# Top-32 attention and a mixture of depths: score blocks turned and masked by half rows, and the order of a step's work on TensorE changed

## The chip, the cores and the metric

The kernel runs on one core of one Trainium2 chip. The core has five engines, each with its own queue of instructions that it works off in order: TensorE (PE in the profile; PEld is its weight loads, which overlap its products), VectorE (DVE), ScalarE (ACT), GpSimd (POOL) and SyncE (SP, which here only starts transfers). They wait for each other through semaphores. TensorE writes into PSUM, eight banks of 512 float32 values for each of 128 partitions; ScalarE and VectorE read those banks, and everything else lies in SBUF. The metric is device time in microseconds (us), as the median of several runs.

## What is computed

Two blocks, one after the other. First attention for 8 batches of 8 heads, 576 positions and 64 channels, in which each query keeps only its 32 largest scores:

```python
scores = scale * np.matmul(q, k.transpose(0, 1, 3, 2))
kth = np.partition(scores, -top_k, axis=-1)[..., -top_k:-top_k + 1]
mask = scores >= kth
scores = np.where(mask, scores, -1000000000.0)
scores = scores - np.max(scores, axis=-1, keepdims=True)
attn = np.exp(scores)
attn = attn / (np.sum(attn, axis=-1, keepdims=True) + 1e-09)
return np.matmul(attn, v).astype(np.float32)
```

The heads of a batch are laid side by side to rows of 512, and then, in each batch, 128 of the 576 rows (those with the largest product with a gate vector) go through a small two-layer network and are added to:

```python
scores = np.einsum('bsd,d->bs', x, w_gate)
out = x.copy()
for b in range(B):
    top_idx = np.argpartition(-scores[b], capacity)[:capacity]
    xe = x[b, top_idx]
    h = np.maximum(xe @ w1, 0.0)
    ye = h @ w2
    g = 1.0 / (1.0 + np.exp(-scores[b, top_idx]))
    out[b, top_idx] = x[b, top_idx] + g[:, None] * ye
```

## The kernel before, in words

The work is cut into units. A unit is one block of 128 queries for two heads (two half blocks of 64 queries for the last 64 positions, where four heads share a unit). A batch has 18 units, the whole problem 144. The scores of a unit, `sc`, are 128 partitions (queries) by 2 heads by 576 keys.

The main loop (line 1108) is a pipeline over units. In its step n five units are in work at once, each in another stage:

- unit n+1: its scores are multiplied on TensorE (`multiply`, line 486) into four PSUM banks and copied to SBUF by ScalarE (`keep`, line 506);
- unit n: VectorE finds a lower bound of the 32nd largest score (`bound_of`, line 1066);
- unit n-1: ScalarE marks what lies below the bound (`sides`, line 554) and GpSimd multiplies scores and marks into `y` (line 1080);
- unit n-2: VectorE finds the 32nd largest itself in `y` (`kth_of`, line 1084);
- unit n-3: `mask_of` (line 1102) writes `less`, bfloat16, which is positive where a score is below the 32nd largest; ScalarE does the first head, GpSimd the second;
- unit n-4: `weigh` (line 1053) turns the scores on TensorE so that keys lie on partitions, ScalarE takes the exponential (`pT`, and `last` for the last 64 keys of both heads), `values` (line 642) multiplies with v into the bank `av`, and `keep_values` (line 674) copies the result to `xs`.

Turning and masking are two products into the same place: a transpose of a 128x128 block of scores, and on top of it a product of `less` with the matrix `out_of_reach`, which has -2^90 on its diagonal, so that what is masked becomes hugely negative before the exponential (`turn_some`, line 608). A unit has eight such blocks, four for each head, in the two banks `tr`, and a ninth (`turn_last`, line 630), in the last 128 columns of the bank `av`, with the last 64 keys of both heads.

Beside this, a step on TensorE carries up to two "half loads" (blocks of the next batch's keys or queries, transposed into spare columns of the score banks, `loads`, line 1169) and, behind the values, a piece of the mixture of an earlier batch (`next(mixtures[b], None)`, line 1219): part of the first layer (`h_ps`), of the second (`y_ps`), or a transpose of the chosen rows (`xe_ps`). ScalarE's part of the mixture (`hT`, `xeT`, `gy`) is put into a list, `late`, which `flush` (line 210) empties right after the step's mask.

The order is written out by hand: each engine runs its instructions in the order of the program text (`InOrder`, line 37, which is why nearly all instructions carry line 45 in the profile). So in one step of the main loop

- TensorE does: eight blocks of turn and mask, the ninth block, the half loads' transposes, the scores of unit n+1, the values of unit n-4, a piece of the mixture;
- ScalarE does: exponential `pT`, exponential `last`, `less`, the list `late`, the copies of the half loads, the copy `sc`, the copy `xs`, `sides` twice.

The first product of the values waits for ScalarE's exponential `last`, since the block that it reads lies in the bank `av` that the values write. All eight PSUM banks are in use: two for `tr`, one for `av`, one for the mixture, four for the scores.

After the loop a hand-written ending (from line 1290) does the same for the last four units without new scores, and then the mixture of the last batch.

Of the kernel before, what the change touches and what calls it, by code (L numbers as in the profile page):

```python
# [10 lines left out]
AF = mybir.ActivationFunctionType  # L11
# [20 lines left out]
J = 4  # L32
# [16 lines left out]
def kernel(  # L49
# [16 lines left out]
    NHP = H // 2  # L66
    NT = J + 1
    JP = J * P
    R = S - JP
# [4 lines left out]
    scale = 1.0 / float(D) ** 0.5 / SMALLER  # L74
# [29 lines left out]
    ident = const.tile([P, P], FP32, name="ident")  # L104
# [132 lines left out]
    class Rows:  # L237
# [67 lines left out]
        def turn_last(self, w, tr):  # L305
            for c in range(NHP):
                pe.transpose(
                    tr[:, c // 2, c % 2 * R : (c % 2 + 1) * R],
                    self.last[w][:, 2 * c : 2 * c + 2, :].rearrange("p h d -> p (h d)"),
                    ident[0:R, 0:R],  # L310
                )
# [14 lines left out]
        def turn(self, i, tr, c0=0, c1=J):  # L326

            for c in range(c0, c1):
                pe.transpose(
                    tr[:, c - c0, :],  # L330
                    self.rows[i][:, c, :, :].rearrange("p h d -> p (h d)"),
                    ident,
                )
            if c1 == J:
                self.fetch()
# [144 lines left out]
    def room_for_scores():  # L480
        return ps_sc.tile([P, 2, 2, 512], FP32, name="ps")
# [21 lines left out]
    def by_head(ps):  # L503
        return [ps[:, i, :, :] for i in range(2)]
# [103 lines left out]
    def turn_some(tr, z, less):  # L608

        pe.transpose(tr, z, ident)  # L610
        if less is not None:
            pe.matmul(
                tr, less, out_of_reach, start=False, stop=True, skip_group_check=True
            )

    def room_to_turn():
        return ps_tr.tile([P, 2, J, P], FP32, name="ptr"), ps_av.tile(
            [P, 512], FP32, name="av"
        )

    def turn(z, tr, less=None):

        for i in range(2):
            for c in range(J):
                at = slice(c * P + i * R, (c + 1) * P + i * R)
                turn_some(
                    tr[:, i, c, :], z[:, i, at], None if less is None else less[:, i, at]
                )

    def turn_last(z, av, less=None):  # L630

# [10 lines left out]
    def values(t, g, pT, last, av, vs):  # L642

        vt, vpair = vs  # L650
        for i, heads in enumerate(heads_of(t, g)):
            for c in range(J):
                for r in (0, R):
                    h = heads[-1 if r else 0][0]
                    pe.matmul(
                        av[r : r + R, i * DE : (i + 1) * DE],
                        pT[:, i, c, r : r + R],
                        vt[:, h, c, :],
                        start=(c == 0 and i == 0),
                        stop=False,  # L660
                        skip_group_check=True,
                    )
        for r in (0, R):
            h = heads_of(t, g)[0][-1 if r else 0][0]
            pe.matmul(
                av[r : r + R, 0 : 2 * DE],
                last[:, r : r + R],
                vpair[:, h // 2, :, :].rearrange("p h e -> p (h e)"),
                start=False,
                stop=True,  # L670
                skip_group_check=True,
            )
# [377 lines left out]
    def is_unit(n):  # L1050
        return 0 <= n < N

    def weigh(sc, tr, av, less):

        turn(sc, tr, less)
        tr_last = turn_last(sc, av, less)
        pT = ptpool.tile([P, 2, J, P], FP32, name="pT")
        last = ptpool.tile([P, P], FP32, name="last")

        def exp():  # L1060
            act.activation(pT, tr, AF.Exp, scale=scale)
            act.activation(last, tr_last, AF.Exp, scale=scale)

        return pT, last, exp

    def bound_of(n):
        b, i = divmod(n, per_batch)
# [40 lines left out]
    for n in range(-1, N):  # L1108
        b, i = divmod(n, per_batch)
        if i == 0 and 0 <= b < B - 1:  # L1110
            qkv[b + 1] = room_for_qkv(b + 1)
            loading = chain(
                loading, Rows(k[b + 1], q[b + 1], *qkv[b + 1][0:2]).parts()
            )
        if 0 < n + 1 < NHP:
            first_pairs.turn(n + 1)
        if n == 0:
            for hp in range(2):
                first_pairs.turn_queries(hp)
            for hp in range(2):  # L1120
                first_pairs.keep_queries(hp)
        if n == NHP - 1:
            for hp in range(2, NHP):
                first_pairs.turn_queries(hp)
            for hp in range(2, NHP):
                first_pairs.keep_queries(hp)
            first_pairs.last_queries()
            first_steps.close()
            ps_sc = all_steps.enter_context(
                tc.tile_pool(name="ps_sc", bufs=1, space=PS)  # L1130
            )
        if n == 1:
            load_v(v[0], qkv[0][2])
        if n == NHP:
            load_weights()


        gating = normalised
        if inverting is not None:
            normalised = inverting[0:2]  # L1140
            vector_late.insert(0, lambda a=inverting: normalise(*a))
            inverting = None
        else:
            normalised = None
        if gating is not None:
            amid_late.append(lambda a=gating: gates(*a))

        if is_unit(n - 4):  # L1150
            tr, av = room_to_turn()
            pT, last, exp = weigh(scs.pop(n - 4), tr, av, masks.pop(n - 4))
            exp()
        if is_unit(n - 3):
            mask_of(n - 3, (act, None) if n in scatter_steps else None)
        flush()
        if is_unit(n + 1):
            b, t, g = units[n + 1]
            kT, qT = qkv[b][0:2]
            b, i = divmod(n, per_batch)  # L1160
            if n + 1 < NHP:
                ps = room_for_first_scores()
                multiply(t, g, kT, qT, ps)
                if is_unit(n - 1):
                    what_is_below(n - 1)
                stay_busy((10, 10, 20, 30)[n + 1])
            else:
                ps = room_for_scores()
                loads = list(islice(loading, first_loads[i] if b == 0 else loads_at[i]))
                halves = [ps[:, a, :, HALF : HALF + P] for a in range(2)]  # L1170
                for load, half in zip(loads, halves):
                    load[0](half)
                multiply(t, g, kT, qT, by_head(ps))
                for load, half in zip(loads, halves):
                    load[1](half)
                if n == NHP - 1:
                    stay_busy(20)
            scs[n + 1] = keep(ps)
        if is_unit(n - 4):
            b4, t4, g4 = units[n - 4]  # L1180
            values(t4, g4, pT, last, av, qkv[b4][2])
            if n in place_steps:
                values_bank[0] = av
                next(mixtures[place_steps[n]])
            if g4 == 0:
                xs = xpool.tile([P, H, DE], FP32, name="xs")
                if t4 == 0:
                    x = xpool.tile([P, NT, HD], FP32, name="x")
                    pg = gates_of[b4 % 2]
                    of_batch[b4] = x, pg  # L1190
            keep_values(t4, g4, av, xs)
            if g4 == groups(t4) - 1:
                inverting = b4, t4, xs
                n4 = R if t4 == J else P
                keep_sums(n4, xs, sums[0:n4, b4 * NT + t4, :])
            while kept:
                kept.pop(0)()


        if is_unit(n):  # L1200
            bound_of(n)
        flush_vector()
        flush_pool()
        if is_unit(n - 2):
            kth_of(n - 2)
        while after_kth:
            after_kth.pop(0)()


        if is_unit(n - 1) and n + 1 >= NHP:  # L1210
            what_is_below(n - 1)

        if gating is not None:
            b, t = gating
            if t == J:
                store(out[b], of_batch[b][0])
                mixtures[b] = mixture(float(b * S), of_batch[b][1], ranks[:, b, :])
        for b in mix_steps.get(n, ()):
            next(mixtures[b], None)
        b, i = divmod(n, per_batch)  # L1220
        if i == v_at and 0 <= b < B - 1:
            load_v(v[b + 1], qkv[b + 1][2])
# [14 lines left out]
    weighed = {}  # L1237
# [2 lines left out]

    def weigh_unit(m):
        tr, av = other_room(m) if (N - m) % 2 else room_to_turn()
        weighed[m] = *weigh(scs.pop(m), tr, av, masks.pop(m)), av

    def values_unit(m):
        pT, last, _, av = weighed[m]
# [371 lines left out]
```

## Time and profile before

| | |
|---|---|
| time, median of 3 runs (lowest to highest) | 814.45 us (814.24 to 816.94) |
| the profiled execution: its time, and its span | 816.28 us, 814.4 us |
| granted TensorE clock, mean | 0.998 |
| busy: PE, PEld | 777.2 us (95%), 600.3 us (74%) |
| busy: DVE, ACT, POOL | 783.5 us (96%), 729.5 us (90%), 721.6 us (89%) |
| 18 steps, from 400.00 to 495.88 us | 95.88 us; DVE busy 95.73, PE 94.83, ACT 91.08, POOL 90.47 |

The time of an execution is that of the slowest core; here there is one. The span runs from its first instruction to its last. A line of the timeline gives the start in us from the beginning of the span, the time taken, the engine, the operation, what it writes and reads, `row x column` sizes, and in brackets the idle time before it with what ended it. Products on TensorE are pipelined: each takes about 0.2 us from start to end, but the next one starts long before; their cost is read from one start to the next. A float32 product appears as two records, a float32 transpose as one. Tile names stand without their numbers: `ptr` is `tr`, `ps` the score banks, `rows` and `last` the loaded keys and queries (but `last<-av` on ScalarE is the exponential of the ninth block).

### The profile page before, as it was taken

How to read it: one execution, taken by the hardware profiler on the slowest of the kernel's cores; microseconds unless marked ns; L12 is line 12 of the kernel's file. 1: busy time of each engine (PE TensorE's matmuls, PEld its weight loads, DVE VectorE, ACT ScalarE, POOL GpSimd, SP SyncE). 2: the span in 40 equal slices, each digit the busy share in tenths (PEclk: the TensorE clock that was granted, in tenths of full speed). 3: DMA queues.
4: the chain of work that ended last, by engine and by line, in shares of the span. 5: the costliest groups of instructions: out<-in, count | busy, mean ns of one | idle time of the engine just before them, and what ended most of it. 6: DMA issues, size and time to landing. Idle time of an engine off the chain costs nothing. (4 is left out here: it accounts for less than half of the span.)

```text
span 814.4 us, 28453 instructions
## 1 busy us (share of the span) xinstructions
PE 777.2 (95%) x10231; PEld 600.3 (74%) x10231; DVE 783.5 (96%) x4655; ACT 729.5 (90%) x1577; POOL 721.6 (89%) x722
## 2 busy tenths in 40 slices
PE   8988888888999999999999999999999999999987
PEld 6766666667887778877787777877788777867756
DVE  6999999999999999999999999999999999999962
ACT  5999999999999999999999999999999999879840
POOL 3899999999999999999999999999999999998921
PEclk9999999999999999999999999999999999999999
DMA  8931214121151123221251221512224102001021
GB/s 169 287 89 28 52 58 106 29 53 28 60 114 26 43 59 90 66 54 33 74 106 29 54 41 60 100 28 54 41 80 94 28 3 79 23 5 25 2 72 30
DMA packets 121732, 50.38 MB, mean 62 GB/s; under 512 B 116016, under 2 KB 116016, under 8 KB 120560
## 3 DMA queue, kind: packets, MB, share of 16 engines
q1 hardware_dynamic: 118368, 43.94, 22.0%
q0 software_dynamic: 1744, 4.20, 2.9%
q8 instruction: 82, 1.34, 0.7%
q14 instruction: 66, 0.54, 0.2%
q10 hardware_dynamic: 1472, 0.36, 0.2%
HBM read 36.93 MB, written 11.55 MB: 60 GB/s over the span
## 5 line engine op out<-in xcount | busy, mean ns | idle before, releaser
L45 POOL TENSOR_TENSOR y<-sc,sides 128x576 f32<-128x576 f32 x288 | 365.8, 1294 | 51.0 <-ACT sides L45 49.3
L45 DVE MAX8 cand<-sc 128x8 f32<-128x82 f32 (+1 forms) x2016 | 314.0, 227 | 4.3 <-ACT sc L45 4.2
L45 POOL TENSOR_SCALAR less<-sc,next 128x576 bf16<-128x576 f32 x135 | 233.2, 1728 | 2.2 <-DVE next L45 1.2
L45 ACT ACTIVATE sides<-sc,bound 128x576 bf16<-128x576 f32 x288 | 223.5, 791 | 0.0
L45 PE MATMUL ptr<-out_of_reach,less 128*128 128x128 bf16 x1136 | 203.3, 219 | 18.0 <-POOL less L45 17.1
L45 PE MATMUL ptr<-ident,sc 128*128 128x128 f32 x1136 | 214.6, 280 | 0.0
L45 DVE MAX8 next<-y 128x8 f32<-128x584 f32 x288 | 204.4, 751 | 0.5 <-POOL y L45 0.5
L45 PEld LDWEIGHTS av<-v,pT 128*64 128x64 f32 x4608 | 146.1, 137 | 65.9 <-ACT last L45 62.6
L45 ACT ACTIVATE pT<-ptr 128x1024 f32<-128x1024 f32 x142 | 145.3, 1024 | 39.5 <-PE ptr L45 38.5
L45 PEld LDWEIGHTS ptr<-ident,sc 128*128 128x128 f32 x1136 | 159.9, 141 | 28.2 <-issue 16.7
L45 PE MATMUL ps<-kT,qT 64*128 64x288 f32 (+1 forms) x1248 | 174.0, 425 | 0.0
L45 PE MATMUL av<-v,pT 128*64 128x65 f32 x4608 | 166.0, 224 | 8.1 <-ACT last L45 7.4
L45 PEld LDWEIGHTS <-less 128*128 128x128 bf16 x1296 | 134.4, 104 | 36.7 <-POOL less L45 24.0
L45 ACT COPY sc<-ps 128x1152 f32<-128x1152 f32 x140 | 159.1, 1137 | 0.0
L45 PEld LDWEIGHTS ps<-kT,qT 64*128 64x128 f32 (+1 forms) x1248 | 95.8, 175 | 34.5 <-issue 20.9
L45 ACT ACTIVATE less<-sc,next 128x576 bf16<-128x576 f32 x141 | 109.8, 779 | 2.9 <-DVE next L45 2.8
L45 DVE MATCH_REPLACE8 cand<-best,cand 128x21 f32<-128x21 f32 (+1 forms) x576 | 98.9, 179 | 0.0
L45 DVE MAX8 best<-cand 128x8 f32<-128x21 f32 (+1 forms) x576 | 90.3, 189 | 0.0
L45 PE MATMUL h_ps<-xeT,w 128*128 128x128 f32 x464 | 65.7, 286 | 0.0
L45 PEld LDWEIGHTS h_ps<-xeT,w 128*128 128x128 f32 x464 | 55.8, 191 | 9.1 <-issue 7.0
L45 ACT ACTIVATION_READ_ACCUMULATOR sides<-sc,bound 128x1 f32 x288 | 61.0, 212 | 0.0
L45 PE MATMUL y_ps<-w,hT 128*128 128x512 f32 x112 | 60.6, 636 | 0.0
(165 smaller groups left out, 908.3 us busy)
## 6 DMA issues: line engine op xcount, KB each, us to landing
v<-in_v_dram SPq DMA_DIRECT2D x64, 128.0 KB, 4.4
out_dram<-x SPq DMA_DIRECT2D x8, 1024.0 KB, 4.0
rows<-in_k_dram SPq DMA_DIRECT2D x56, 128.0 KB, 2.9
rows<-in_q_dram SPq DMA_DIRECT2D x56, 128.0 KB, 3.0
w<-in_moe_w_dram SPq DMA_DIRECT2D x2, 2048.0 KB
gate_row<-row_dram SPq DMA_DIRECT2D x7, 288.0 KB, 4.4
last<-in_q_dram SPq DMA_DIRECT2D x8, 128.0 KB, 3.3
vpair<-in_v_dram SPq DMA_DIRECT2D x16, 64.0 KB, 3.9
```

Of the source, the lines that this page charges most:

```text
L45: return lambda *a, **kw: self._tc.keep_in_program_order(fn(*a, **kw))
```

## The change

Three things are changed, in three functions and in the main loop.

First, `turn` no longer takes a block of 128 queries whole. Each block is turned as two halves of 64 queries, partitions 0 to 63 and 64 to 127, each against its own 64x64 corner of the identity; then each half is masked with its own 64x64 corner of `out_of_reach`. A unit's eight blocks were 8 transposes and 8 masks with 128 moving columns, and are now 16 and 16 with 64 moving columns, in the order: first half turned, second half turned, first half masked, second half masked. The halves go to different PSUM banks: `by_half` reads the two banks as one for each half of the queries (before: one for each head). `values` reads the exponentials through the same view; the exponential itself is unchanged. The ninth block stays whole.

Second, the ninth block is taken out of `weigh` into a function of its own, `turn_rest`, and is turned after the scores of unit n+1. ScalarE's exponential `last` moves with it: it stood before `less` and the list `late`, and now stands behind both.

Third, the half loads' transposes, which stood before the scores of unit n+1, now follow the scores and the ninth block. So TensorE's order in a step is: eight blocks by halves, scores, ninth block, half loads, values, mixture. ScalarE's is: `pT`, `less`, `late`, `last`, half loads' copies, `sc`, `xs`, `sides`.

In the ending after the loop, blocks are turned by halves too, but the ninth block still follows at once.

```diff
+    def by_half(a):
+        return a.rearrange("p r c (b i) -> p r (c b) i", i=R)
+
     def turn(z, tr, less=None):
+        to = by_half(tr)
+        halves = [slice(r * R, (r + 1) * R) for r in range(2)]
         for i in range(2):
             for c in range(J):
                 at = slice(c * P + i * R, (c + 1) * P + i * R)
-                turn_some(
-                    tr[:, i, c, :], z[:, i, at], None if less is None else less[:, i, at]
-                )
+                for r, q in enumerate(halves):
+                    pe.transpose(to[:, r, i * J + c, :], z[q, i, at], ident[q, q])
+                for r, q in enumerate(halves):
+                    if less is not None:
+                        pe.matmul(
+                            to[:, r, i * J + c, :],
+                            less[q, i, at],
+                            out_of_reach[q, q],
+                            start=False,
+                            stop=True,
+                            skip_group_check=True,
+                        )
...
                     pe.matmul(
                         av[r : r + R, i * DE : (i + 1) * DE],
-                        pT[:, i, c, r : r + R],
+                        by_half(pT)[:, r // R, i * J + c, :],
                         vt[:, h, c, :],
...
     def weigh(sc, tr, av, less):
         turn(sc, tr, less)
-        tr_last = turn_last(sc, av, less)
         pT = ptpool.tile([P, 2, J, P], FP32, name="pT")
         last = ptpool.tile([P, P], FP32, name="last")
         def exp():
             act.activation(pT, tr, AF.Exp, scale=scale)
-            act.activation(last, tr_last, AF.Exp, scale=scale)
-        return pT, last, exp
+
+        def turn_rest():
+            tr_last = turn_last(sc, av, less)
+            return lambda: act.activation(last, tr_last, AF.Exp, scale=scale)
+
+        return pT, last, exp, turn_rest
...
                 ps = room_for_scores()
+                multiply(t, g, kT, qT, by_head(ps))
+        if is_unit(n - 4):
+            turn_rest()()
+        if is_unit(n + 1):
+            if n + 1 >= NHP:
+                b, i = divmod(n, per_batch)
                 loads = list(islice(loading, first_loads[i] if b == 0 else loads_at[i]))
                 halves = [ps[:, a, :, HALF : HALF + P] for a in range(2)]
                 for load, half in zip(loads, halves):
                     load[0](half)
-                multiply(t, g, kT, qT, by_head(ps))
                 for load, half in zip(loads, halves):
                     load[1](half)
```

More of the change, by code (lines that the diff above doesn't have):

```diff
@@ L1151 @@
             tr, av = room_to_turn()
-            pT, last, exp = weigh(scs.pop(n - 4), tr, av, masks.pop(n - 4))
+            pT, last, exp, turn_rest = weigh(scs.pop(n - 4), tr, av, masks.pop(n - 4))
             exp()
@@ L1159 @@
             kT, qT = qkv[b][0:2]
-            b, i = divmod(n, per_batch)
             if n + 1 < NHP:
@@ L1242, in weigh_unit, with both @@
         tr, av = other_room(m) if (N - m) % 2 else room_to_turn()
-        weighed[m] = *weigh(scs.pop(m), tr, av, masks.pop(m)), av
+        pT, last, exp, turn_rest = weigh(scs.pop(m), tr, av, masks.pop(m))
+        exp_rest = turn_rest()
+        def both():
+            exp()
+            exp_rest()
+        weighed[m] = pT, last, both, av
     def values_unit(m):
```

## The prediction

> **What bounds the kernel now.** I read the page's busy line first, then the windows over one batch, then the timeline of one step for TensorE and ScalarE, then the totals of the waits.
>
> ```profile
> PE 777.2 (95%) x10231; PEld 600.3 (74%) x10231; DVE 783.5 (96%) x4655; ACT 729.5 (90%) x1577; POOL 721.6 (89%) x722
> ...
> 400.00:495.88 95.88, 94.83 (x1262) 73.38 (x1263) 95.73 (x577) 91.08 (x198) 90.47 (x88) 1.00 0.27 60
> ```
>
> These are busy us of PE, PEld, DVE, ACT and POOL; the second line is one batch of 18 steps, 5.33 us a step. VectorE has 0.15 us of idle time in it, so no change elsewhere can make a batch much shorter than VectorE's own work. But VectorE isn't alone. One step on TensorE, then on ScalarE:
>
> ```profile
> 413.46 1.16 PE L45 MATMUL h_ps<-xeT,w 128*128 128x128 f32 x8
> 414.45 0.27 PE L45 MATMUL ptr<-ident,sc 128*128 128x128 f32 x1
> 414.56 0.22 PE L45 MATMUL ptr<-out_of_reach,less 128*128 128x128 bf16 x1
> 414.62 0.28 PE L45 MATMUL ptr<-ident,sc 128*128 128x128 f32 x1
> ...
> 415.76 0.22 PE L45 MATMUL ptr<-out_of_reach,less 128*128 128x128 bf16 x1
> 415.81 0.28 PE L45 MATMUL av<-ident,sc 128*128 128x128 f32 x1
> ...
> 415.99 0.39 PE L45 MATMUL ps<-ident,rows 128*128 128x128 f32 x2
> 416.30 1.24 PE L45 MATMUL ps<-kT,qT 64*128 64x288 f32 x8
> 417.47 1.15 PE L45 MATMUL av<-v,pT 128*64 128x65 f32 x32
> 418.46 0.39 PE L45 MATMUL av<-vpair,last 128*64 128x130 f32 x4
> 418.78 1.05 PE L45 MATMUL h_ps<-xeT,w 128*128 128x128 f32 x7
> ```
>
> ```profile
> 416.02 1.02 ACT L45 ACTIVATE pT<-ptr 128x1024 f32<-128x1024 f32 x1 [0.50 <-PE ptr L45]
> 416.94 0.27 ACT L45 ACTIVATE last<-av 128x128 f32<-128x128 f32 x1
> 417.09 0.78 ACT L45 ACTIVATE less<-sc,next 128x576 bf16<-128x576 f32 x1
> 417.76 0.38 ACT L45 ACTIVATE hT<-h_ps 128x256 f32<-128x256 f32 x1
> 418.02 0.39 ACT L45 ACTIVATE qT<-ps 128x256 f32<-128x256 f32 x1
> ...
> 419.28 0.31 ACT L45 COPY xs<-av 128x130 f32<-128x130 f32 x1
> ```
>
> TensorE goes through the step without a pause: the values start (417.47) when the scores have streamed, and ScalarE's `last`, which they need, was done at 417.21. ScalarE waits 0.50 us for the turned blocks. So TensorE sets the step (5.29 to 5.33 us in most), with VectorE level with it.
>
> ```profile
> PEld av L45 <- ACT last L45: 62.6, 133, 1.3
> ...
> ACT pT L45 <- PE ptr L45: 38.5, 83, 1.4
> ```
>
> The pair of waits is a ring: turned blocks, exponential, values, mixture, next turned blocks. Before, it has about 0.26 us of slack in this step (417.21 to 417.47).
>
> **The change, part by part.** Halving the turn. A block costs 0.171 us now (414.45 to 414.62), 0.114 for the transpose and 0.057 for the mask. The nearest row for a half is the load of the last keys, 64 rows and 64 moving columns:
>
> ```profile
> 399.93 0.40 PE L45 MATMUL ps<-ident,last 64*128 64x64 f32 x3
> 400.11 0.51 PE L45 MATMUL ps<-kT,qT 64*128 64x288 f32 x1
> 400.17 0.22 PE L45 MATMUL ps<-ident,last 64*128 64x64 f32 x1
> ```
>
> In the trace their starts are 0.061 us apart once running, and the first is 0.113 before the second, so an uncovered weight load of this shape costs 0.052. A product on the other half rows (400.11) starts in the midst of them and does not slow them: the two halves of the array run side by side. So both transposes take 0.061 together. The masks stream 64 of 128 columns, 0.028 of 0.057. If streaming alone counts, a block costs 0.061 + 0.028 = 0.089 us. But the next transpose's weights can load only beside the mask before it, and 0.052 doesn't fit under 0.028: then 0.061 + 0.053 = 0.114. If the halves do not run side by side, it is 2 x (0.061 + 0.028 to 0.057) = 0.18 to 0.24, more than now. I take 0.114, nearest to the rows with both loads and products in them. Turning then costs 0.91 us a unit and not 1.37: TensorE saves 0.46 us a step. The Trainium skill, "TensorE: Matmul & The Clock Gate", section "LDWEIGHTS (loading the stationary operand)", speaks against this: a load's time goes by its columns alone, 107 ns for 128 of them however few the rows, and its section on weight-path modes has bfloat16 loads go two elements at a time, 53 ns; in a block's two loads that would be 0.160 us and the sum below would end near 877 us. The row shows 61 ns for load and product of such a half together, and the measurement decides.
>
> Switches. From a product on 128 rows to one on 64 rows, 0.09 us are lost (the second `rows` transpose starts at 416.10, its slot of 0.11 ends at 416.21, the scores start at 416.30), and the first weight load is bare, 0.05. Before, this stands ahead of the scores; now the scores follow the turn without it, but the turn follows the mixture with it, +0.14 on the ring, and the one ahead of the ninth block lies in TensorE's wait for `last`.
>
> Moving `last` on ScalarE. Its exponential now stands behind `less` (0.67 us, 417.09 to 417.76) and the late list (`hT` 0.26, 417.76 to 418.02). In the changed program the first product of the values still waits for it. So this wait replaces the one on TensorE's own queue. Behind it on TensorE stand 36 records of values, the mixture piece and the next turn; and ScalarE waits for the values at `xs`. The ninth block and the half loads fit into the gap: turn 0.91, scores 1.0, switch, block and mask 0.37 with 0.25 of latency end 2.5 us after the turn's start, ScalarE asks for it at 1.10 + 0.92 + 0.67 = 2.69. The half loads' transfers come no later than before; SP and POOL are passed by nothing.
>
> The ring after, from the exponential `pT`: 0.92 to the next instruction, `less` 0.67, `last` with handover 0.32 (in the step before it ran at 406.50 and the values began at 406.82), values and `h_ps` up to the next turn 1.31 + 0.99 = 2.30, switch 0.14, turn 0.91, 0.19 until `pT` starts (1.57 - 8 x 0.171 = 0.20 now). Sum 5.45 us with nothing late, 5.71 with `hT`; now 5.32. ScalarE's own ring, if it waits for `xs`: 0.92 + 0.67 + 0.32 + 1.40 (values) + 0.16 + 1.67 (`sides` twice) = 5.14, plus 0.25 with `keep_sums`, plus what is late.
>
> By kinds over the 18 steps from 405.58 on, each with its own rows: three steps with `h_ps` alone gain 0.14 each; three with `h_ps` and `hT` go from 5.11, 5.33 and 5.32 to 5.72, +1.40; one with `y_ps` and `hT` +0.40; three with `y_ps` +0.14 each; two with two half loads -0.04 together; one with the places' products +0.35; one with `g` late +0.23; one with `gy` late +0.30 and one with 64-row copies +0.25 (both on ScalarE's ring); one with `xe_ps` +0.02; one with `xeT` and `bounded` late +0.63. Sum +4.38, 95.9 to 100.3 us. Over the 90 steps from 203 us on: 22.4 (five times 4.38, 0.5 more where the last batch is packed closer); the 15 steps behind them, with up to two pieces each, +7.4 by the same rule. Together +29.8.
>
> The first 30 steps have no mixture on TensorE; the same rule gives them 1.2 us less than they take, so VectorE and GpSimd bound them. I count 0, with -1 to +3 as ends. VectorE takes up the first 1.5 us: its first maximum on a unit starts 1.5 to 3 us after the copy `sc`. The ending has four units turned in TensorE's own time: 0.46 less, 0.14 more for a switch, three in a row on the path: -0.9.
>
> The profiled execution took 816.28 us (span 814.4), 1.83 over the median. 816.28 + 29.8 - 1.5 - 0.9 = 843.7, so 842 as a median.
>
> **Rivals.** First, on the other side: TensorE's busy time alone decides. It falls from 5.32 to 5.14 us a step, and then VectorE is the bound, which can give back only what GpSimd costs it: its 40 products for the gates take 0.95 us at the median and 0.68 at best, 40 x 0.27 = 11 us at most. That gives 803 to 810. It needs the ring below 5.3, for which a block may cost no more than 0.095 us in steps with nothing late and 0.06 with `hT`; streaming alone (0.089) does not reach that in a third of the steps. Against it: `last` is behind `less` in the program.
>
> Second, the halves don't run side by side, or their loads queue: 0.18 us a block makes the same sum +81, 893 us; 0.15 makes it +57, 869. Against it: the row at 400.11.
>
> Third, no change: at 0.06 us a block, loads wholly hidden, the sum is +4.8 - 2.4, 817 us, with ScalarE's ring as bound.
>
> Streaming alone (0.089) gives +14.1 - 2.4, 826; it belongs to my forecast's mechanism.
>
> **How the numbers follow.** I give 0.70 to the late `last` with blocks of 0.08 to 0.13 us (820 to 855), 0.12 to slower blocks (above 855), 0.12 to no change within 0.5% (4 us, about what a measurement of this kernel can tell), 0.06 to faster. The range reaches from 816, the case of blocks at 0.06, to 862, blocks at 0.14, and leaves out the fastest and the slowest cases. Faster 0.06, same 0.12, slower 0.82.
>
> **What would show it.** PE's own idle time ahead of the values, put down to ACT `last`, is 7.4 us in all now and rises to 20 or more; the values start 1.9 us after `pT`, 2.2 with `hT`; eight blocks take 0.9 us; VectorE gets idle time, for `sc` or `y`, of 25 us or so. Wrong would be: values that start before `less` ends, VectorE still without idle time, or a block over 0.13 us.

## The result, and the profile after

The changed kernel takes 849.59 us (median of 4 runs, 848.57 to 850.53) beside 814.43 us for the kernel before, a ratio of 1.0424 with a 95% interval of 1.0400 to 1.0448. It is slower by 35 us; the forecast was 842, with a range of 816 to 862. The profiled execution took 849.98 us, with a span of 848.1 us and a mean granted clock of 0.998.

The busy line of its page and the windows over one batch (18 steps) answer to the first lines of before; the columns are busy us of PE, PEld, DVE, ACT and POOL, then the granted clock:

```profile
PE 740.1 (87%) x12535; PEld 550.6 (65%) x12535; DVE 801.5 (95%) x4655; ACT 741.2 (87%) x1577; POOL 721.9 (85%) x722
...
404.46:504.91 100.45, 91.00 (x1551) 66.85 (x1551) 98.64 (x577) 92.67 (x199) 90.28 (x88) 1.00 0.24 58
```

A batch takes 100.45 us and not 95.88. TensorE works 3.8 us less in it than before (91.00, was 94.83) and so has 9.45 us of idle time, where it had 1.05. VectorE, which had 0.15 us of idle time in a batch, has 1.81, so no engine is quite full any more, and the time lies in waits. One step on TensorE in the changed kernel's timeline:

```profile
421.63 0.25 PE L45 MATMUL ptr<-ident,sc 64*128 64x64 f32 x2
421.72 0.19 PE L45 MATMUL ptr<-out_of_reach,less 64*128 64x64 bf16 x2
421.75 1.22 PE L45 MATMUL ps<-kT,qT 64*128 64x288 f32 x8
422.90 0.33 PE L45 MATMUL av<-ident,sc 128*128 128x128 f32 x1
423.07 0.22 PE L45 MATMUL av<-out_of_reach,less 128*128 128x128 bf16 x1
423.12 0.39 PE L45 MATMUL ps<-ident,rows 128*128 128x128 f32 x2
423.87 1.15 PE L45 MATMUL av<-v,pT 128*64 128x65 f32 x32 [0.36 <-ACT last L45]
424.85 0.39 PE L45 MATMUL av<-vpair,last 128*64 128x130 f32 x4
425.17 1.16 PE L45 MATMUL h_ps<-xeT,w 128*128 128x128 f32 x8
426.26 0.27 PE L45 MATMUL ptr<-ident,sc 64*128 64x64 f32 x2
```

and the same step on ScalarE:

```profile
421.96 1.03 ACT L45 ACTIVATE pT<-ptr 128x1024 f32<-128x1024 f32 x1 [0.35 <-PE ptr L45]
422.88 0.77 ACT L45 ACTIVATE less<-sc,next 128x576 bf16<-128x576 f32 x1
423.55 0.27 ACT L45 ACTIVATE last<-av 128x128 f32<-128x128 f32 x1
423.70 0.37 ACT L45 COPY kT<-ps 128x256 f32<-128x256 f32 x1
423.95 1.14 ACT L45 COPY sc<-ps 128x1152 f32<-128x1152 f32 x1
425.29 0.27 ACT L45 COPY xs<-av 128x130 f32<-128x130 f32 x1 [0.19 <-PE av L45]
```

The scores have streamed early, and the ninth block is done at 423.29 (its mask starts at 423.07 and takes 0.22), a quarter of a microsecond before ScalarE gets to it at 423.55; until then ScalarE is busy with `less`. The values start (423.87) 0.32 us after `last` does (423.55), the same handover as before. From `pT` that is 1.91 us; in the next step, where `hT` stands ahead of `last`, it is 2.18. The totals of the waits say the same over the whole span (us in total, times, longest):

```profile
PEld av L45 <- ACT last L45: 122.4, 140, 2.1
PE av L45 <- ACT last L45: 89.6, 129, 1.9
POOL y L45 <- ACT sides L45: 81.3, 94, 10.1
...
ACT xs L45 <- PE av L45: 36.6, 123, 2.1
ACT pT L45 <- PE ptr L45: 29.9, 73, 1.2
DVE next L45 <- POOL y L45: 16.5, 27, 3.9
```

Two of them before the change:

```profile
PE av L45 <- ACT last L45: 7.4, 16, 1.1
...
ACT xs L45 <- PE av L45: 2.0, 5, 0.7
```

The step is now a ring of two engines that wait for each other: TensorE for `last`, ScalarE for the values at `xs` and for the turned blocks at `pT`.

### The profile page after: what moved, and what is told of

Its sections match the earlier page's. It is cut to its first block, busy times and chain, and to the rows that moved or that the text cites. A ratio compares the mean times of both kernels' runs of the same rounds, so it can differ in the third digit from the quotient of the medians.

```text
span 848.1 us, 33207 instructions
## 1 busy us (share of the span) xinstructions
PE 740.1 (87%) x12535; PEld 550.6 (65%) x12535; DVE 801.5 (95%) x4655; ACT 741.2 (87%) x1577; POOL 721.9 (85%) x722
## 5 line engine op out<-in xcount | busy, mean ns | idle before, releaser
L45 POOL TENSOR_TENSOR y<-sc,sides 128x576 f32<-128x576 f32 x288 | 376.1, 1330 | 84.9 <-ACT sides L45 81.3
L45 PE MATMUL av<-v,pT 128*64 128x65 f32 x4608 | 166.5, 224 | 90.7 <-ACT last L45 89.6
L45 ACT ACTIVATE sides<-sc,bound 128x576 bf16<-128x576 f32 x288 | 220.5, 769 | 0.0
L45 PE MATMUL ps<-kT,qT 64*128 64x288 f32 (+1 forms) x1248 | 170.2, 422 | 0.0
L45 PEld LDWEIGHTS ptr<-ident,sc 64*128 64x128 f32 x2272 | 137.3, 137 | 47.4 <-issue 40.7
L45 PEld LDWEIGHTS <-less 64*128 64x128 bf16 (+1 forms) x2448 | 160.8, 131 | 8.5 <-POOL less L45 7.1
L45 PE MATMUL ptr<-ident,sc 64*128 64x64 f32 x2272 | 159.0, 252 | 0.0
L45 PE MATMUL ptr<-out_of_reach,less 64*128 64x64 bf16 x2272 | 146.2, 189 | 5.7 <-POOL less L45 5.6
L45 PEld LDWEIGHTS ps<-kT,qT 64*128 64x128 f32 (+1 forms) x1248 | 93.0, 176 | 17.0
L45 ACT COPY xs<-av 128x130 f32<-128x130 f32 (+1 forms) x160 | 43.1, 269 | 37.0 <-PE av L45 36.6
```

The source lines that it names most:

```text
L45: return lambda *a, **kw: self._tc.keep_in_program_order(fn(*a, **kw))
```

## The experiments

Nine runs of eight kernels. Where a ratio is given, the kernel before ran beside them on the same chip (814.8 to 815.0 us).

**One part of the change alone: halves, old order.** The kernel before with the new `turn`, `by_half` and the line in `values`, and nothing else of the diff.

```diff
+    def by_half(a):
+        return a.rearrange("p r c (b i) -> p r (c b) i", i=R)
     def turn(z, tr, less=None):
...
-                turn_some(
-                    tr[:, i, c, :], z[:, i, at], None if less is None else less[:, i, at]
-                )
+                for r, q in enumerate(halves):
+                    pe.transpose(to[:, r, i * J + c, :], z[q, i, at], ident[q, q])
...
-                        pT[:, i, c, r : r + R],
+                        by_half(pT)[:, r // R, i * J + c, :],
```

> The kernel before with the turn by halves alone; ninth block, half loads, scores and the exponential last stay in the old order. Theory (the late exponential last makes the ring longer): a block is 0.12 us and not 0.171, two more switches of 0.14 us, so TensorE's step falls from 5.32 to about 5.15 us and VectorE sets the step: 806 to 816 us, VectorE idle under 3 us from 100 to 700 us. Rival 1 (the halves themselves cost, through twice the instructions and the 64-row mode): over 830 us. Rival 2 (the half loads' transposes behind the scores delay the score copy): as the theory, since they stay ahead here.

Measured: 809.21 us, ratio 0.9931 (0.9914 to 0.9947). A second time, later: 809.83, ratio 0.9935 (0.9917 to 0.9953).

> The kernel before with the turn by halves alone, run beside the next kernel on the same chip: 808 to 811 us, as its first run had it.

The windows over one batch of the first run, in the columns of above:

```profile
392.76:487.23 94.47, 92.46 (x1552) 67.83 (x1551) 94.33 (x576) 91.26 (x199) 89.72 (x88) 1.00 0.27 61
```

The half rows are no loss at all: they make the kernel 0.65% faster. VectorE has 0.14 us of idle time in 94.47, so it is the bound, and this is the time that the rival "TensorE's busy time alone decides" forecast, 803 to 810. It and its variant with grouped masks, below, are the fastest kernels of the study. But VectorE was as full before (0.15 us idle in a batch). What the kernel gains is therefore mostly VectorE's own time: its 40 products for the gates take 4.5 us less, of the 6.5 us between the two profiled spans (814.4 and 807.9). Before, and here:

```profile
L45 DVE CUSTOM_DVE_ANT_0 prod<-x,wg 128x512 f32<-128x512 f32 (+1 forms) x40 | 42.2, 1056 | 0.2
L45 DVE CUSTOM_DVE_ANT_0 prod<-x,wg 128x512 f32<-128x512 f32 (+1 forms) x40 | 37.7, 942 | 0.2
```

TensorE works 2.4 us less in a batch (94.83 to 92.46), and the batch gets 1.4 us shorter, as much as VectorE's work in it does (95.73 to 94.33).

**The other part alone: new order, whole blocks.** The changed kernel with the old `turn`.

```diff
-                for r, q in enumerate(halves):
-                    pe.transpose(to[:, r, i * J + c, :], z[q, i, at], ident[q, q])
...
+                turn_some(
+                    tr[:, i, c, :], z[:, i, at], None if less is None else less[:, i, at]
+                )
```

> The changed kernel with whole blocks turned again: the new order alone. Theory: the ring gets 8 x 0.0535 us longer and loses one switch of 0.14, +0.29 us a step in some 101 steps, 872 to 886 us, with values that start 1.9 us after the exponential pT (2.2 with hT late). Rival 1: without the halves the loss goes, 812 to 830 us. Rival 2: about the 850 us of the changed kernel.

Measured: 880.57 us, ratio 1.0807 (1.0786 to 1.0829). The values start 1.91 and 2.18 us after `pT`, as in the changed kernel, and the steps of the same batch take 5.77 and 6.05 us in place of 5.47 and 5.75. So beside whole blocks the order costs 66 us, and the halves give 31 of them back: 0.30 us a step, where the turn lies on the ring. With the old order the halves could give only what VectorE leaves. The loss is the order's.

**Which part of the order: `last` first.** The scores, the ninth block and `last` are issued ahead of `less` and of the late list. TensorE's order stays that of the changed kernel; on ScalarE `last` follows `pT` again.

```diff
             exp()
+        if is_unit(n + 1) and n + 1 >= NHP:
+            b, t, g = units[n + 1]
+            kT, qT = qkv[b][0:2]
+            ps = room_for_scores()
+            multiply(t, g, kT, qT, by_head(ps))
+        if is_unit(n - 4):
+            turn_rest()()
         if is_unit(n - 3):
             mask_of(n - 3, (act, None) if n in scatter_steps else None)
         flush()
...
-            else:
-                ps = room_for_scores()
-                multiply(t, g, kT, qT, by_head(ps))
-        if is_unit(n - 4):
-            turn_rest()()
```

> The changed kernel, but the scores, the ninth block and the exponential `last` are issued ahead of `less` and of the late list, so that ScalarE does `last` straight after `pT`; TensorE's order stays. Theory (the place of `last` on ScalarE sets the step): values start 1.6 us after `pT` in all steps, not 1.9 and 2.2, TensorE no longer waits 122 us for `last`. The wait moves to ScalarE, about 0.4 us a step for the ninth block (which is done 1.1 us after `pT` starts, with 0.2 of latency, where `pT` ends at 0.92): ScalarE's 5.03 us of work a step and this wait make 5.43 if nothing else is waited for, 5.6 with the wait for the values as now; 826 to 850. Rival (TensorE's new order costs the time, wherever `last` stands on ScalarE): the values start as late as before and the time stays at 846 to 853.

Measured: 816.08 us (10 runs), ratio 1.0014 (1.0005 to 1.0024): 33.5 of the 35 us are gone, with TensorE's new order untouched, the place of the half loads included. The mechanism is the theory's, the rival falls, and the expected size (826 to 850) was missed on the good side. Beside the halves with the old order (809.21) 6.9 us remain. Its ScalarE timeline, and then two totals of its waits:

```profile
420.10 1.05 ACT L45 ACTIVATE pT<-ptr 128x1024 f32<-128x1024 f32 x1
421.30 0.28 ACT L45 ACTIVATE last<-av 128x128 f32<-128x128 f32 x1 [0.15 <-PE av L45]
421.47 0.77 ACT L45 ACTIVATE less<-sc,next 128x576 bf16<-128x576 f32 x1
```

```profile
PE av L45 <- ACT last L45: 22.0, 51, 1.0
ACT last L45 <- PE av L45: 23.9, 88, 0.4
```

The values (421.62) start 1.52 us after `pT` here, and 1.2 to 1.7 over a batch. I expected ScalarE to wait 0.4 us a step for the ninth block; it waits 0.15 here, and 0.27 at the mean of its 88 waits. In this step TensorE is ahead and `pT` no longer waits for the turn (no idle time before it; 0.35 in the changed kernel). VectorE is full again, 95.36 us of a batch's 95.50:

```profile
405.58:501.08 95.50, 91.63 (x1549) 67.11 (x1549) 95.36 (x577) 91.53 (x199) 90.55 (x88) 1.00 0.25 61
```

**The late list behind `last`.** In the changed kernel `flush()` is moved behind the ninth block; `less` stays ahead of `last`.

```diff
             mask_of(n - 3, (act, None) if n in scatter_steps else None)
-        flush()
...
         if is_unit(n - 4):
             turn_rest()()
+        flush()
```

> The changed kernel with the late list (hT, xeT, gy, g) emptied behind the exponential last, and less still ahead of it. Theory: the ring loses hT's 0.27 us in the steps that have it (5.75 to 5.48), and most of xeT's and gy's 0.6 us: about 2 us in 18 steps, 12 to 14 us in all, 835 to 839 us. Rivals 1 and 2: no difference, 848 to 852 us.

Measured: 839.7 us, ratio 1.0296 (1.0279 to 1.0313), 9.9 us less than the changed kernel, where 12 to 14 were expected. The steps with `hT` in the traced batch now take 5.47 us (5.75 in the changed kernel), and `less` still keeps them there. But the 9.9 us are not a clean price of the late list. Of the 8.6 us between the two traced spans (848.1 and 839.5) 1.5 lie in the ending, where the clock does not fall in this kernel (see the last experiment). And the traced batch gains almost nothing (100.38 us, 100.45 in the changed kernel), since its 17th and 18th steps take 5.85 and 6.47 us (5.60 and 5.25 in the changed kernel). In the 18th TensorE waits 1.51 us for `last`, and then its granted clock, the third number from the end of the row, is halved:

```profile
498.64:502.05 3.41, 3.41 (x49) 2.74 (x46) 3.38 (x19) 2.61 (x7) 1.71 (x1) 0.50 0.00 0
```

In the next batch, at full clock, the 18th step takes 5.25. Why the 17th is longer (5.9 to 6.1 us in three other batches too) was not followed. So what `less` and the late list cost apart is known only roughly; what they cost together, 33.5 us, is shown by the experiment before.

**The ninth block first.** The changed kernel, but the ninth block is turned ahead of the eight and `last` follows `pT`; the half loads stay behind the scores.

```diff
     def weigh(sc, tr, av, less):
+        tr_last = turn_last(sc, av, less)
         turn(sc, tr, less)
...
             act.activation(pT, tr, AF.Exp, scale=scale)
+            act.activation(last, tr_last, AF.Exp, scale=scale)
...
-        if is_unit(n - 4):
-            turn_rest()()
```

> The changed kernel with the ninth block turned ahead of the eight, and the exponential last straight behind pT again, ahead of less; halves, and half loads behind the scores, as in the changed kernel. Theory: TensorE's step is about 4.9 us, ScalarE's 5.1 to 5.2 and VectorE's 5.33, so VectorE sets it: 804 to 815 us; against it only that the ninth block needs GpSimd's less 0.5 us sooner, which can cost up to 5 us in the first 30 steps. Rival 1: over 830 us. Rival 2: over 835 us, since the half loads stand behind the scores here.

Measured: 825.83 us, ratio 1.0145 (1.0126 to 1.0164): neither what my theory expected nor what the rivals did. The values do start early, 1.31 us after `pT`, and a third of a batch's steps take 5.09 to 5.12 us. But a turn that begins with the ninth block needs both heads' masks and a free `av` bank at once. Of its waits, and then one turn of it on TensorE:

```profile
PE av L45 <- ACT xs L45: 32.5, 49, 1.3
PE av L45 <- POOL less L45: 22.3, 41, 0.8
```

```profile
411.05 0.33 PE L45 MATMUL av<-ident,sc 128*128 128x128 f32 x1
411.83 0.23 PE L45 MATMUL av<-out_of_reach,less 128*128 128x128 bf16 x1 [0.45 <-POOL less L45]
411.99 0.28 PE L45 MATMUL ptr<-ident,sc 64*128 64x64 f32 x2
```

Here the eight blocks stand behind a mask that GpSimd finished at 411.77; in the order of before, the second head's masks come half a turn later. Such steps take 5.6 to 5.8 us, and a batch 97 us; nearly 5 us more go in the first 34 units (their end is at 207.79 us, 202.99 before the change). Some of that may be the clock: it is granted at half from 121.21 to 124.62 us and from 196.30 to 199.72, which it was not before the change; how much the waits and how much the clock cost there was not separated. An early `last` is worth what the block's own inputs allow.

**What makes a block cost 0.1175 us: masks grouped.** In the changed kernel each head's four pairs of half transposes run first, and then its four pairs of half masks.

```diff
         for i in range(2):
-            for c in range(J):
-                at = slice(c * P + i * R, (c + 1) * P + i * R)
+            ats = [slice(c * P + i * R, (c + 1) * P + i * R) for c in range(J)]
+            for c, at in enumerate(ats):
                 for r, q in enumerate(halves):
                     pe.transpose(to[:, r, i * J + c, :], z[q, i, at], ident[q, q])
+            for c, at in enumerate(ats):
                 for r, q in enumerate(halves):
```

> The changed kernel, but each head's four pairs of half transposes run first and its four pairs of half masks behind them. It tells what makes a block cost 0.1175 us. Theory of the prediction (the load of the next transpose's weights does not fit under the mask's 0.028 us): among themselves the transposes run at 0.061 us a pair and the masks at 0.03 to 0.053, eight blocks take 0.71 to 0.91 us in place of 0.94, and the time falls by 3 to 25 us, to 825 to 846. Rival (the half mask's own load is the slow part, 0.088 us from the transposes to the mask in the trace of the changed kernel): transposes at 0.061 or less, masks at 0.06 to 0.09 a pair, eight blocks 0.95 to 1.2 us, 850 to 876.

Measured: 837.27 us, ratio 1.0275 (1.0256 to 1.0293), 12.3 us less than the changed kernel. A unit's turn in it:

```profile
432.47 0.46 PE L45 MATMUL ptr<-ident,sc 64*128 64x64 f32 x8
432.76 0.28 PE L45 MATMUL ptr<-out_of_reach,less 64*128 64x64 bf16 x8
432.88 0.44 PE L45 MATMUL ptr<-ident,sc 64*128 64x64 f32 x8
433.16 0.28 PE L45 MATMUL ptr<-out_of_reach,less 64*128 64x64 bf16 x8
433.27 0.49 PE L45 MATMUL ps<-kT,qT 64*128 64x288 f32 x2
```

From the first transpose to the scores it takes 0.81 us, and 0.965 in the changed kernel. In the single records of the trace, transposes follow each other at 0.062 us a pair and masks at 0.029, and the two halves of a pair start 0.003 to 0.006 us apart. A pair of each is thus 0.091; 0.029 more is lost at each return from masks to a transpose (432.852 for the last pair of masks, 432.881 and 432.972 for the next two pairs of transposes). The changed kernel pays nearly that in every block: 0.091 + 0.027 is 0.1175 within the rounding. The loss thus lies at the return from a mask to a transpose and not in the half mask's own load, which costs nothing among masks: the rival falls. That it is the transpose's load which does not fit under a mask of 0.029 agrees with it; another cost of going from bfloat16 masks back to float32 transposes would look the same and was not tested.

**Is the halves' kernel bound by VectorE?** The kernel with halves alone, with the masks grouped in the same way.

```diff
         for i in range(2):
-            for c in range(J):
...
+            for c, at in enumerate(ats):
                 for r, q in enumerate(halves):
                     pe.transpose(to[:, r, i * J + c, :], z[q, i, at], ident[q, q])
+            for c, at in enumerate(ats):
```

> The kernel before with the turn by halves, each head's four pairs of transposes ahead of its four pairs of masks (old order of everything else). The turn takes 0.81 us and not 0.965, as in the changed kernel with grouped masks. Theory (with `last` early, VectorE is the bound: 99.84 of 100 us busy with the halves alone): TensorE's 0.16 us a step is worth nothing, 806 to 811 us, VectorE busy over 99.7 of 100 us. Rival (TensorE's ring still sets steps beside VectorE): 0.16 us a step over 140 steps, 22 us, or a good part of it: 787 to 803.

Measured: 809.8 us, ratio 0.9928 (0.9907 to 0.9950), beside 809.83 for the halves alone on the same chip. TensorE's busy time falls from 752.0 to 735.2 us and nothing comes of it; VectorE stays full:

```profile
400.00:500.00 100.00, 94.85 (x1641) 69.44 (x1638) 99.86 (x608) 96.12 (x210) 94.06 (x92) 1.00 0.26 64
```

The saving that was worth 12 us where the turn lies on the ring is worth nothing under a full VectorE.

**The ending: TensorE kept at work.** In the changed kernel's step for the unit with `pT` at 797.6 us there are no scores left, and TensorE waits 1.91 us for `last`. Here it is given 32 products that nobody reads. (The expectation places them ahead of the ninth block; they stand behind it.)

```diff
         if is_unit(n - 4):
-            turn_rest()()
+            rest = turn_rest()
+            if not is_unit(n + 1):
+                spare = room_for_scores()
+                for _ in range(32):
+                    pe.matmul(spare[:, 0, 0, 0:P], out_of_reach, out_of_reach)
+            rest()
```

> The changed kernel, but in the one step that has no scores left to compute (pT at 797.6 us) TensorE is given 32 bfloat16 products that nobody reads, between the turned blocks and the ninth block. There it waits 1.9 us for `last`, and the granted clock in the next 4.7 us is 0.62 to 0.69. Theory (the lull brings the clock down): the clock stays above 0.9 there, the values of that unit take 0.93 to 1.0 us and not 1.29, and from that `pT` to the end it takes 48.6 to 49.2 us in place of 50.48. Rival (the clock falls there anyway): 50.2 to 50.7 us, clock below 0.75.

Measured: 848.6 us (one run, span 846.8). The windows of the changed kernel, then of this one, with the granted clock as above:

```profile
797.00:799.80 2.80, 0.90 (x22) 0.59 (x18) 2.34 (x18) 2.13 (x4) 2.80 (x4) 1.00 0.00 0
799.80:801.20 1.40, 1.40 (x34) 1.40 (x35) 1.40 (x4) 0.00 (x0) 0.84 (x1) 0.69 0.00 0
801.20:804.50 3.30, 3.30 (x24) 2.96 (x21) 0.67 (x2) 2.62 (x8) 1.44 (x2) 0.62 0.02 5
800.32:803.73 3.41, 3.41 (x35) 3.07 (x32) 1.55 (x5) 1.85 (x6) 0.99 (x2) 0.50 0.02 5
```

```profile
797.00:799.80 2.80, 2.80 (x66) 2.71 (x62) 2.32 (x19) 1.88 (x4) 2.80 (x4) 1.00 0.00 0
799.80:801.20 1.40, 1.28 (x39) 1.10 (x37) 1.40 (x3) 0.25 (x2) 1.16 (x1) 1.00 0.00 0
801.20:804.50 3.30, 3.30 (x55) 2.93 (x52) 0.98 (x4) 2.97 (x8) 1.79 (x2) 1.00 0.03 5
```

The last row of the changed kernel lies across the two above it: there the clock is halved. Here it stays at full speed. From the start of that unit's values to the next turn it takes 3.29 us and not 4.87, and from its `pT` to the end 48.85 and not 50.47 (48.66 before the change). The lull brings the clock down, and that costs 1.6 us. This is read from one traced execution of each kernel; the whole time alone would not show it, as 848.6 lies within the changed kernel's runs (848.57 to 850.53).

## Why the prediction was right, point by point

The sign, the mechanism and the range held; the point was 7.6 us low. By its steps (times from the traced executions of before and after):

- *`last` behind `less` and the late list.* Right, within 0.04 us: values 1.91 and 2.18 us after `pT` (forecast 1.9 and 2.2), steps 5.47 and 5.75 (forecast 5.45 and 5.71). The runs show it as the cause: with `last` back behind `pT` and TensorE's order as changed, 33.5 of the 35 us are gone.
- *A block at 0.114 us.* It took 0.1175. Its terms were near (grouped masks): 0.062 for the transposes (0.061), 0.029 for the masks (0.028), and the loss at the next transpose is 0.027, where I took the pair of half masks to vanish in a load of 0.053 (0.061 + 0.053); 0.062 + 0.029 + 0.027 is the same sum counted the other way. The halves run side by side (starts 0.003 to 0.006 us apart), so the second rival falls. The Trainium skill, "TensorE: Matmul & The Clock Gate", section "LDWEIGHTS (loading the stationary operand)", would have had a load of 128 float32 columns at 107 ns. Among themselves two such loads with their products took 62 ns here, so the measurement decides against it.
- *The switch to half rows, 0.14 us.* Between `h_ps` and the first transpose lie 0.206 us; with whole blocks, 0.112. So 0.094, and some 0.02 more until the first mask: close to 0.12.
- *A batch +4.38.* It took +4.57 (100.45 against 95.88). The 90 steps from unit 34 on took +23.56 (forecast 22.4), the 15 behind them +7.72 (7.4).
- *The first 30 steps 0; VectorE absorbs 1.5 us.* Up to 203 us the change costs +0.56. The absorption of 1.5 us does not show: the later steps grew by more than was forecast, and not by less. A likely reason is that VectorE was already full before the change, so that it had no slack to take up; no run tests it. This also corrects a reading of the lines before: TensorE alone did not set the step there. With the halves alone TensorE's work fell by 2.4 us a batch, and the batch by 1.4, to VectorE's own work.
- *The ending -0.9.* The largest miss: from unit 139's `pT` to the end +1.81. The sum had no term for the clock, and 1.62 of the miss is the halved clock; without it, +0.2. What I counted as three shorter turns on the path did not show either; why, no run tells.
- Together, against a sum of +27.4 for the profiled execution: 0.56 + 31.28 + 1.81 = 33.65 us, which is the difference of the spans (848.09 - 814.44). The terms thus miss by 6.3 us; the other 1.3 come from the 1.83 us taken off at the end, since the changed kernel's traced execution lies only 0.4 over its median.
- *What would show it.* PE's own idle time put down to ACT `last` went from 7.4 to 89.6 us (forecast: 20 or more), eight blocks took 0.94 us (0.9), TensorE's busy share fell from 95 to 87%. VectorE's new idle time was 25 us in the forecast and is 15.7 in the trace (848.1 - 801.5 = 46.6, against 30.9). Its busy time grew by 18.0 us, 12.8 of them in the 40 products for the gates, 42.2 us before and 55.0 after. These longer products are not what made the kernel slow: with the masks grouped they took as long (55.6) and the time fell by 12.3 us, and with the order alone they took 40.2 and the time was 880.57.
- *Rivals.* "TensorE's busy time alone decides" had the right price (803 to 810), and the condition that it named, a ring below 5.3 us, is what separates the two: with `last` early, the halves' kernel has many steps of 5.13 to 5.17 us. I had this case as one of small chance for the change, and it is the time of one of its parts.

## What to carry to other kernels

A step that is moved on one engine moves its partner on the other: here the ninth block went later on TensorE, where there was room, and its exponential slid behind 0.67 to 0.93 us of other work on ScalarE, where there was none, and the values behind it waited. Take a change of several parts apart before judging it: alone, one part gave 0.65%, the other cost 8%. And a saving shows on the ring that sets the step (0.16 us in most steps and 12.3 in all for the grouped masks) and comes to nothing under an engine that is full (0).

## What the runs showed of the hardware beyond that

- A wait of 1.91 us, in a stretch where TensorE worked 0.90 of 2.80 us, was followed by a granted clock of 0.50 from 800.32 to 803.73 us. With the late list behind `last`, a wait of 1.51 us was followed by 0.50 from 498.64 to 502.05. The Trainium skill, "TensorE: Matmul & The Clock Gate", section "Part 1: The HAM clock gate", has the clock fall after an idle window of some 3.4 us; here less was enough. Waits of 0.36 us a step, all through the loop, left it at 1.00. These rows give no threshold: in the changed kernel 1.5 us of idle time between 404.43 and 407.84 us were not followed by a lower clock.
- Half masks of 64 rows and 64 columns follow each other at 0.029 us a pair, loads of fresh weights included.
- VectorE's 40 products for the gates take between 0.66 and 4.28 us each, 37.7 us in all in the halves' kernel, 42.2 before, 55.0 after, 61.6 with the late list behind `last`. Of those above 1 us 13 of 14 before and 27 of 28 after lie beside GpSimd's product `y`, but 21 of the 26 shorter ones before do too, so what decides is left open. They are most of what still differs between two kernels that VectorE bounds: 809.21 with 37.7 us, 816.08 with 42.2.
